# Attention and experts on one core: the experts' operations in an order read from a table, and the cast of the slots in five parts

## The chip, the cores and the metric

The program runs on one core of a Trainium2 chip. The metric is the device time of one execution in microseconds (us); lower is better. The unchanged kernel was timed three times: 1247.51, 1247.69 and 1257.23 us, median 1247.69 us.

## The reference

The program computes an attention and then a mixture of experts on its output. Queries are averaged in pairs, so 576 pooled queries meet 1152 keys, for 8 batches of 8 heads of width 64. The output, seen as 4608 tokens of width 512, goes to 8 experts. Every expert takes exactly 4608 / 8 = 576 tokens, handed out greedily from the highest gate logit down.

```python
q_pool = q.reshape(B, H, S // 2, 2, D).mean(axis=3)
attn = softmax(scale * q_pool @ k.T) @ v
x = attn.transpose(0, 2, 1, 3).reshape(4608, 512)
logits = x @ w_gate                     # 4608 x 8
for idx in argsort(-logits.flatten()):  # token idx // 8, expert idx % 8
    if token not assigned and counts[expert] < 576: assign it
for e in range(8):
    out[mask_e] = relu(x[mask_e] @ w1[e]) @ w2[e]   # 512 -> 1024 -> 512
```

## The kernel before

The program has two parts, one after the other. The attention works on 32 pairs of heads; its instructions are put in order by the class Timed, which reads a place for every operation from a table TIME. At its end VectorE (DVE) also builds the constants that the experts need. They are made by routing_tables, and one of them is slots, the numbers 0 to 639 in every row, cast from whole numbers to 16-bit floats in one instruction (L493, recorded by the helper at L475). Each of these constant operations has the tag tb and a place of its own in TIME, one every 12.98 us of the table's time.

The experts follow one another, k = 0 to 7. For each of them the kernel does three things.

**Routing** (route, L1249 to L1482). The next expert to be filled and its 576 tokens are found by a search over sorted keys in eight rounds. A round goes to and fro between DVE and TensorE (PE): DVE compares (GE, L1276), PE counts (rt<-W,GE, L1282), DVE picks its own counts (dg, red, L1285, L1287), PE adds them up (L1291), DVE compares with the room left and narrows the search (L1295 to L1301). After the rounds PE adds up once more (L1327), DVE closes the expert (L1333 to L1344) and sums (PS, tot, L1360, L1363), PE makes offsets (L1368 to L1371), DVE writes four step tables (ST, L1411), PE looks the tokens up (L1416), DVE turns that into indices (hit, idx, L1423, L1427). What the next expert's search needs is brought up to date by a count of the tokens taken (WG, ng on DVE, L1464, L1466; then PE, L1468), by U (L1476 to L1480) and by W (L1268, L1269). The routing of an expert needs the one before to be finished, so the eight of them form one chain. While expert k multiplies, the routing of expert k + 2 runs beside it.

**Fetching** (fetch). GpSimd (POOL) issues the transfers that gather by index: W1 (2 MB, L1557), five blocks of tokens (XG, L1562) and W2 (2 MB, L1557). For experts 2 to 7 DVE transposes the token blocks (XB, L1522), SyncE (SP) issues 16 small transfers that put them in place (L1529), ScalarE (ACT) and POOL split them into a high and a low 16-bit half (Xh L1541 and L1543, Xl L1547). The weights are split in the same way: ACT scales them by a power of two and casts (L1622, L1626), POOL subtracts (L1632).

**Multiplying** (ffn). PE makes 16 groups of 12 matmuls (ph, L1648), two column ranges for each of eight blocks of the hidden layer, in four banks of PSUM that are used in turn. Each group is read by ACT (relu, HX, L1653) and by DVE (the rest of it, HX, L1657, L1660). Then PE makes the output in five row blocks of 16 or 24 matmuls (po, L1675, L1678); ACT and for the last block DVE move it to SBUF (L1683 to L1689), and POOL scatters it to memory (L1695).

Every engine executes its instructions strictly in the order in which the program lists them. In the experts this order is made by the class Order. Its emit is a list scheduler: it keeps a clock for each engine, takes durations from the od.add calls, waiting times from EOWN and EWAIT, and wherever several operations could start it takes the one with the smaller priority. The priority is the operation's nominal place plus a number for its tag from ELEAD; ELATE makes a tag's result late. Matmuls of ph and po are separate operations here, so a routing instruction may stand in the middle of a group.

Tags that the change and the rows speak of: cmp (compare), pc (PE's count), own, pt (PE's sum), fa and fl (narrow), p8 (PE's last sum), cl, me, px (closing), pf (offsets), st (step tables), pl (look up), ix (indices), tk, p9 (tokens taken, and PE's count of them, L1468), lf, se, ar (CAPS, U, W), mm (ph), re (relu), rs (rest of it), m2 (po), ot, pu (output and scatter), dw, dx, dv (fetch W1, tokens, W2), xb (transpose tokens). A number ahead is the expert, a number behind counts: 3pc4 is the fifth count of expert 3.

The step that the change replaces, and the scheduler's last lines:

```python
    od = Order(ELEAD, ELATE)
    od.OWN, od.WAIT, od.switch = EOWN, EWAIT, 95
```

Of the kernel before, what the change touches and what calls it, by code (L numbers as in the profile page):

```python
# [42 lines left out]
EOWN = {"PE": 0, "ACT": 140, "DVE": 120, "POOL": 130, "SP": 60}  # L43
# [7 lines left out]
class Order:  # L51
# [10 lines left out]
    def __init__(self, lead={}, late={}):  # L62
        self.items, self.lead, self.late = [], lead, late
        self.of, self.cur, self.kind, self.stick, self.early, self.lock = [], None, [], 0, (), []
        self.switch = 83
# [97 lines left out]
class Timed(Order):  # L163
# [21 lines left out]
    def emit(self):  # L185
# [31 lines left out]
        assert done == n  # L217


AT = {"load": -15.5, "vload": -0.5, "split": -13.0, "spread": 0.5, "val": 4.0, "vs": 3.5, "vh": 5.0, "vd": 3.0, "mm":  # L220
      -3.5, "cw": 0.5093, "fold0": 3.5, "fold1": 13.1, "aug": 13.9, "lag": 3, "np": 10, "nm": 9, "stick": 0.5, "nx":
      3, "wu": 50, "pd": [11], "wv": 65, "pd0": [3, 4, 8, 9, 10, 17], "sp": 0, "d1": 2.5, "cw1":
# [217 lines left out]
def routing_tables(nc, pool, ident, jp, scratch, do):  # L440

    J = NBLK
    V = nc.vector

    def one(shape, dt, name):
        return pool.tile(shape, dt, name=name)

    C = dict(ident=ident, before=one([128, 128], BF, "before"), upto=one([128, 128], BF, "upto"),
             ones=one([128, 128], BF, "mones"), e8=one([128, J, E], BF, "e8"), pcol=one([128, 1], F32, "pcol"), pcole=one([128, 1], F32, "pcole"),
             nib=one([128, 5, 16], F32, "nib"), diag=one([128, 64], F16, "diag"), same16=one([128, 128], F16, "same16"),  # L450
             slots=one([128, 640], F16, "slots"), slot1=one([128, 5], F32, "slot1"), jval=one([128, J], F32, "jval"),
             zero=one([128, J], F32, "zero"), TAB=one([128, 2, J + 2], F16, "TAB"), pcol2=one([128, 2], F32, "pcol2"))
    it = {}
    at = 0
    for name, n in (("e8", J * E), ("p", 1), ("pe", 1), ("16", 16), ("d", 64), ("m", 128), ("s", 640), ("s1", 5), ("p2", 2)):
        it[name] = scratch[:, at:at + n]
        at += n
    it8 = it["e8"].rearrange("p (j e) -> p j e", e=E)

    def count(dur, ap, pattern, base, step):  # L460
        do("POOL", dur, lambda: nc.gpsimd.iota(ap, pattern=pattern, base=base, channel_multiplier=step))

    count(480, it8, [[0, J], [-1, E]], E, 0)
    count(80, it["p"], [[0, 1]], 0, 1)
    count(80, it["pe"], [[0, 1]], 128 * E, 1)
    count(80, it["p2"], [[1, 2]], 256 * E, 2)
    count(100, it["16"], [[1, 16]], 1, 0)
    count(210, it["d"], [[-16, 8], [0, 8]], 0, 1)
    count(240, it["m"], [[-1, 128]], 128, 1)
    count(660, it["s"], [[1, 640]], 0, 0)  # L470
    count(90, it["s1"], [[128, 5]], 1, 1)
    do("POOL", 210, lambda: (nc.gpsimd.memset(C["ones"], 1.0), nc.gpsimd.memset(C["zero"], 0.0)))

    def by(dur, f, *a, **k):
        do("DVE", dur, lambda: f(*a, **k))  # L475

    by(130, V.tensor_scalar, C["before"], jp, 0.0, None, op0=OP.is_gt)
    by(130, V.tensor_scalar, C["upto"], jp, 0.0, None, op0=OP.is_ge)
    by(220, V.tensor_copy, C["e8"], it8)
    by(62, V.tensor_copy, C["pcol"], it["p"])  # L480
    by(62, V.tensor_copy, C["pcole"], it["pe"])
    by(62, V.tensor_copy, C["pcol2"], it["p2"])
    by(62, V.memset, C["nib"], 3e9)
    for t in range(4):
        by(70, V.tensor_scalar, C["nib"][:, t, :15], it["16"][:, :15], float(16 ** t), None, op0=OP.mult)
    by(70, V.tensor_scalar, C["nib"][:, 4], it["16"], -1.0, None, op0=OP.add)
    k1 = scratch.bitcast(F32)[:, at:at + 64]
    by(90, V.tensor_scalar, k1, it["d"], 0.0, None, op0=OP.is_ge)
    by(90, V.tensor_scalar, C["diag"], it["d"], 16.0, None, op0=OP.is_lt)
    by(130, V.tensor_tensor, C["diag"], C["diag"], k1, op=OP.mult)  # L490
    by(130, V.tensor_scalar, it["m"], it["m"], 15, None, op0=OP.bitwise_and)
    by(130, V.tensor_scalar, C["same16"], it["m"], 0.0, None, op0=OP.is_equal)
    by(400, V.tensor_copy, C["slots"], it["s"])  # L493
    by(62, V.tensor_copy, C["slot1"], it["s1"])
    by(90, V.tensor_scalar, C["jval"], it["s"][:, :J], 128.0, None, op0=OP.mult)
    for z in range(2):
        by(62, V.tensor_copy, C["TAB"][:, z, J + 1:J + 2], it["p"])
    return C


def attention(ctx, tc, top, kb, sx, kt, qt, v, wg, x_dram, L, npair=NPAIR):
# [549 lines left out]
    for n in range(1, npair, 2):  # L1051
# [8 lines left out]
        else:  # L1060
# [13 lines left out]

LT = {"dve": 0, "pe": 0, "x": 8000, "w": 9900, "w0": 3700, "w1": 8000, "x0": 3000, "zd": 0, "kd": 2, "cs": 4, "wn": 4,
      "xm": 7500, "xp": 4}
ELEAD = {"ar": 4.9, "be": 51.6, "bo": 2.8, "cl": 28.5, "cmp": 29.1, "dv": 1.5, "dw": -46.1, "dx": -41.8,
# [5 lines left out]
ELATE = {"ar": -300, "bo": -300, "cl": -300, "cmp": 150, "dv": 1900, "dw": 750, "dx": 1500, "fa": -150, "fl": -300,  # L1083
# [4 lines left out]


def experts(ctx, tc, top, kb, sx, x_dram, L, w1, w2, out, C):  # L1090
    nc = tc.nc
    const = ctx.enter_context(tc.tile_pool(name="moe_const", bufs=1))
    psum = ctx.enter_context(tc.tile_pool(name="moe_psum", bufs=1, space=PSUM))
    od = Order(ELEAD, ELATE)
    od.OWN, od.WAIT, od.switch = EOWN, EWAIT, 95
    J = NBLK

    def one(shape, dt, name):
# [65 lines left out]
    re = early([128, 1], F32, "re")  # L1164
# [22 lines left out]
    ws = [x.bitcast(F32)[:, 1:2] for x in we]  # L1187
# [12 lines left out]
    rb, tb = rt[:, :128], rt[:, 128:]  # L1200
    ph = [[psum.tile([128, 512], F32, name=f"ph{i}{h}") for h in range(2)] for i in range(2)]
    po = [psum.tile([128, 512], F32, name=f"po{i}") for i in range(2)]
    V = nc.vector
# [433 lines left out]
    def ffn(k, t):  # L1637
        i = k
        for f in range(8):
            fs = slice(128 * f, 128 * f + 128)  # L1640
            for hf in range(2):
                qn = 320 if hf else 256
                qs = slice(256 * hf, 256 * hf + qn)
                p = ph[f % 2][hf][:, :qn]
                xk = [y for x in ("XH", "XL") for y in xkeys(x, 256 * hf, 256 * hf + qn)]
                for z, (d, a, b) in enumerate((d, a, b) for d in range(4) for a, b in ((W1h, Xh), (W1h, Xl), (W1l, Xh))):
                    def mm(fs=fs, qs=qs, p=p, z=z, d=d, a=a, b=b):
                        nc.tensor.matmul(p, a[:, d, fs], b[:, d, qs], start=z == 0, stop=z == 11)  # L1648
                    od.add(t + 0.5, "PE", 138 if hf else 111, mm, r=xk + [(x, f // 2, y) for x in ("W1H", "W1L") for y in range(2)],
                           w=[("ph", f % 2, hf)], tag="mm")  # L1650

                def relu(qs=qs, f=f, p=p):
                    nc.scalar.activation(HH[:, f, qs], p, AF.Relu)  # L1653

                def rest(hf=hf, qs=qs, f=f, p=p):
                    h = HH.bitcast(F32)[:, f, qs]
                    V.scalar_tensor_tensor(HL[:, f, 64 + 256 * hf:320 + 256 * hf], p[:, :256], 0.0, h[:, :256],  # L1657
                                           op0=OP.max, op1=OP.subtract)
                    if hf:
                        V.scalar_tensor_tensor(HL[:, f, :64], p[:, 256:], 0.0, h[:, 256:], op0=OP.max, op1=OP.subtract)  # L1660
                pk, hk = [("ph", f % 2, hf)], [("HH", f, hf)]
                od.add(t + 0.5, "ACT", 334 if hf else 282, relu, r=pk, w=hk, tag="re")
                od.add(t + 0.5, "DVE", 470 if hf else 335, rest, r=pk + hk, w=[("HL", f, hf)], tag="rs")
# [97 lines left out]
```

## Time and profile before

| | us |
|---|---|
| median of three runs | 1247.69 |
| the profiled execution | 1246.02 |
| its span, first to last instruction | 1243.9 |
| PE busy | 1178.5 |
| DVE busy | 986.0 |
| POOL busy | 897.3 |
| ACT busy | 867.1 |

The profiled execution took 1246.02 us, and its span on the core is 1243.9 us. Times below count from the first instruction of that span. The attention runs to 750 us, the experts from there on. PE is the busiest engine; an engine that waits while PE is fed costs nothing. [...]

### The profile page before, as it was taken

The page shows a single profiled execution, that of the slowest core. Times are in us where ns is not written, and L with a number is a line of the kernel's source. Part 1 is how long each engine was busy: PE and PEld are TensorE (multiplying, and loading weights), DVE is VectorE, ACT ScalarE, POOL GpSimd, SP SyncE. Part 2 cuts the span into 40 slices and gives each one's busy share as a digit, 9 for nine tenths or more (in the row PEclk, how much of TensorE's full clock was granted, in tenths as well). Part 3 has the DMA queues.
Part 4 walks back from the last instruction along what each step waited for, and adds up shares of the span by engine and source line. Part 5 has one row for each costly group of instructions (what it writes and reads, how often), then busy time and mean ns, then how long its engine had stood idle before and what let it go on. Part 6 is the DMA issues. An engine that isn't in the chain of part 4 may idle for free.

```text
span 1243.9 us, 37266 instructions
## 1 busy us (share of the span) xinstructions
PE 1178.5 (95%) x14875; PEld 808.1 (65%) x14875; DVE 986.0 (79%) x2323; ACT 867.1 (70%) x1603; POOL 897.3 (72%) x913
## 2 busy tenths in 40 slices
PE   8899999999999999999999996899889999999998
PEld 5566666665666666666666674676667677787776
DVE  8999999999999999999999837888776767761320
ACT  6787887886887878788788660647556464667631
POOL 4688888888788888888887980456475756668641
PEclk8899999999999999999999998999899999999999
DMA  7564675666465576567565300542443436253411
GB/s 224 146 180 122 159 180 138 168 162 146 126 168 140 153 179 159 124 163 181 136 171 128 94 2 20 174 184 83 133 157 120 152 108 215 86 183 118 141 39 38
DMA packets 95692, 171.07 MB, mean 138 GB/s; under 512 B 17694, under 2 KB 54558, under 8 KB 93342
## 3 DMA queue, kind: packets, MB, share of 16 engines
q1 hardware_dynamic: 82574, 107.09, 32.0%
q0 software_dynamic: 12800, 61.58, 16.5%
q8 instruction: 117, 1.92, 0.6%
q14 instruction: 57, 0.47, 0.1%
q10 hardware_dynamic: 144, 0.02, 0.0%
HBM read 99.63 MB, written 18.87 MB: 95 GB/s over the span
## 4 chain that ended last, share of the span: by engine, by line
PE 67%; DVE 19%; issue 5%; ACT 3%; DMA 2%; POOL 2%; another core or an unknown queue 0%; SPq 0%; POOLq 0%; DVEq 0%; ACTq 0%
PE av L872 13%; PE po L1678 12%; PE ph L1648 9%; DVE MX L739 6%; PE sc L838 6%; PE sc L839 6%; PE mt L746 5%; PE kb L838 3%; PE kb L839 3%; PE av L908 3%; DVE PM L860 1%; PE mt L935 1%; POOL W2L L1632 1%; DVE V L689 1%; DMA out_dram<-OT,idx 1%
## 5 line engine op out<-in xcount | busy, mean ns | idle before, releaser
L860 POOL TENSOR_TENSOR PM<-P 128x512 f16<-128x512 f32 x537 | 586.1, 1159 | 114.8 <-ACT P L855 105.2
L739 DVE TENSOR_REDUCE MX<-mt 128x2 f32<-128x1024 f32 (+2 forms) x341 | 374.2, 1131 | 17.9 <-PE mt L746 12.3
L872 PEld LDWEIGHTS <-P 128*128 128x128 bf16 x4608 | 230.1, 98 | 61.0 <-issue 27.2
L855 ACT ACTIVATE P<-sc 128x512 f32<-128x512 f32 x384 | 224.4, 604 | 44.8 <-PE sc L839 40.5
L872 PE MATMUL av<-V,P 128*128 128x65 f16 (+1 forms) x4608 | 243.6, 193 | 1.1 <-DVE X L922 0.6
L872 PE MATMUL av<-V,PM 128*128 128x65 f16 x2304 | 235.5, 195 | 0.7 <-DVE KS L625 0.5
L872 PEld LDWEIGHTS <-PM 128*128 128x128 f16 x2304 | 212.2, 97 | 1.4 <-DVE PM L860 0.6
L839 PE MATMUL sc<-QB,KB 66*128 66x64 f16 (+2 forms) x768 | 178.5, 287 | 0.0
L838 PE MATMUL sc<-QA,KA 128*128 128x512 f16 (+1 forms) x768 | 177.1, 287 | 0.6 <-ACT P L855 0.3
L1678 PE MATMUL po<-W2H,HX 128*128 128x512 f32 x512 | 168.9, 405 | 0.7 <-DVE OT L1688 0.7
L855 ACT ACTIVATE P<-kb 128x512 f32<-128x512 f32 x192 | 115.1, 600 | 62.9 <-PE kb L839 61.4
L1648 PE MATMUL ph<-Xh,W1h 128*128 128x320 f16 (+1 forms) x512 | 147.4, 288 | 2.1 <-DVE HX L1657 1.0
L838 PEld LDWEIGHTS <-KA 128*128 128x128 f16 x1152 | 96.5, 98 | 79.2 <-issue 40.9
L1648 PE MATMUL ph<-Xl,W1h 128*128 128x320 f16 (+1 forms) x512 | 147.5, 288 | 0.5 <-DVE Xl L1512 0.5
L1648 PE MATMUL ph<-Xh,W1l 128*128 128x320 f16 (+1 forms) x512 | 147.4, 288 | 0.0
L1657 DVE SCALAR_TENSOR_TENSOR HX<-ph,HX 128x256 fp32r<-128x256 f32 x128 | 53.2, 419 | 102.4 <-ACT HX L1653 98.9
L1678 PE MATMUL po<-W2L,HX 128*128 128x512 f32 (+1 forms) x320 | 127.9, 400 | 0.0
L1632 POOL TENSOR_TENSOR W1l<-W,W1h 128x512 f16<-128x512 f32 x62 | 72.1, 1165 | 77.2 <-ACT W1h L1626 74.0
L1653 ACT ACTIVATE HX<-ph 128x256 fp32r<-128x256 f32 (+1 forms) x128 | 51.5, 409 | 103.6 <-PE ph L1648 96.0
L1648 PEld LDWEIGHTS <-W1h 128*128 128x128 f16 x1024 | 99.1, 98 | 35.3 <-issue 9.8
L839 PEld LDWEIGHTS <-KB 66*128 66x128 f16 (+1 forms) x1152 | 94.9, 98 | 37.3 <-issue 2.4
L1678 PEld LDWEIGHTS po<-W2H,HX 128*128 128x128 f32 x512 | 94.4, 190 | 17.6 <-DVE OT L1688 1.1
(270 smaller groups left out, 2279.2 us busy)
## 6 DMA issues: line engine op xcount, KB each, us to landing
KD<-in_kt_dram SPq DMA_DIRECT2D x64, 288.0 KB
VD<-in_v_dram SPq DMA_DIRECT2D x32, 576.0 KB
QA<-QH SPq DMA_DIRECT2D x128, 72.0 KB
KA<-KH SPq DMA_DIRECT2D x64, 144.0 KB
KB<-KH SPq DMA_DIRECT2D x64, 144.0 KB
KA<-KL SPq DMA_DIRECT2D x64, 144.0 KB
x_dram<-X SPq DMA_DIRECT2D x16, 576.0 KB
QS<-in_qt_dram SPq DMA_DIRECT2D x31, 288.0 KB
```

The lines of the kernel that those rows point to most:

```text
L739: od.add(t, "DVE", d, lambda: nc.vector.tensor_reduce(dst, src, axis=AX.X, op=OP.max), r=[f"m{m}"], w=w, tag="mr", k=z)
L746: nc.tensor.matmul(mt[s][:, y], pairs[b][s], KH[i][h, ks], start=True, stop=True)
L838: nc.tensor.matmul(c, KA[i][:, s, ks], QA[i][:, s, qs], start=first, stop=False, skip_group_check=True)
L839: nc.tensor.matmul(c, KB[i][:kr, s, ks], QB[i][:kr, s, qs], start=False, stop=last, skip_group_check=True)
L855: od.add(g + 0.1, "ACT", 480, lambda: nc.scalar.activation(p, c, AF.Exp, scale=1.0 / UNIT), r=[ck], w=[("P32", g % NP)], tag="exp", k=g % ...
L860: od.add(g + 0.2, en, dur, lock=1, fn=lambda: eng.tensor_tensor(pm, p, hi, op=OP.subtract), r=[("P32", g % NP)], w=[("PM", g % NM)], tag=" ...
L872: nc.tensor.matmul(out, w[:, qs], v, start=kb == 0 and j == 0 and y == 0, stop=kb == NKB - 1 and y == 2, skip_group_check=True)
L1632: eng.tensor_tensor(o, a, b, op=OP.subtract), r=[key] + sr + [(nm + "H", z, y)], w=[(nm + "L", z, y)], first=first, lock=1, tag="wl" if nm ...
L1648: nc.tensor.matmul(p, a[:, d, fs], b[:, d, qs], start=z == 0, stop=z == 11)
L1653: nc.scalar.activation(HH[:, f, qs], p, AF.Relu)
L1657: V.scalar_tensor_tensor(HL[:, f, 64 + 256 * hf:320 + 256 * hf], p[:, :256], 0.0, h[:, :256], op0=OP.max, op1=OP.subtract)
L1678: nc.tensor.matmul(o[:n], a[:, z, q0:q0 + n], b[:, z], start=z == 0 and y == 0, stop=z == 7, skip_group_check=True)
```

## The change

The class Order is replaced, for the experts, by a class Listed. It collects the operations by name. A name is the expert, the tag and a running number; the 12 matmuls of a ph group have one name, and 6 matmuls of po have one name, so these now stay together. The operations are then emitted in the order of their numbers in the table ETIME, except that none is emitted before the operations it depends on. ELEAD and ELATE go. One line of the table stands in the diff as an example (the place of 5mm15 is on its next line):

```diff
+class Listed(Order):
+    def add(self, t, eng, dur, fn, r=(), w=(), late=0, first=0, tag=None, kind=0, lock=None, k=None):
+        Order.add(self, t, eng, dur, fn, r, w, late, first, tag, kind, lock, k)
+        self.names.append((int(t // 10), tag or {"PE": "pe", "DVE": "dv", "POOL": "po", "ACT": "ac", "SP": "sp"}[eng] + "_"))
+
+    def emit(self):
...
+            name = f"{k}{tag}{z // {'mm': 12, 'm2': 6}.get(tag, 1)}"
...
+        heap = [(self.table[made[i][0]], i) for i in range(n) if not left[i]]
+        heapq.heapify(heap)
...
+            _, i = heapq.heappop(heap)
+            for fn in made[i][1]:
+                fn()
...
-    by(400, V.tensor_copy, C["slots"], it["s"])
+    for c in range(5):
+        by(100, V.tensor_copy, C["slots"][:, 128 * c:128 * c + 128], it["s"][:, 128 * c:128 * c + 128])
...
+         346253, "5re13": 354527, "5rs13": 355006, "5mm14": 347909, "5re14": 354861, "5rs14": 355476, "5mm15":
...
-    od = Order(ELEAD, ELATE)
-    od.OWN, od.WAIT, od.switch = EOWN, EWAIT, 95
+    od = Listed(ETIME)
```

In the attention, the cast of slots is now five instructions of 128 columns. TIME gets four more places (2tbw to 2tbz), so the five casts stand one every 12.98 us of the table's time, and the four small constants behind them move back by four places. The rest of the attention keeps its order.

In the experts all engines are reordered. Three places follow, each before and after. A name in capitals is a tile; the number after an underscore tells apart tiles of one kind; numbers behind a name are its shape.

First DVE, where it gets the routing of expert 3 ready while expert 1 multiplies. HX with 128x256 or 128x64 is the rest of a ph group of expert 1, W is what PE's first count of expert 3 needs beside GE, GE is the compare. Before:

```order
L1660 SCALAR_TENSOR_TENSOR HX<-ph_14630,HX 128x64
L1230 TENSOR_REDUCE kb<-T_14555 128x36
L1471 TENSOR_TENSOR CAPS<-CAPS,rt 128x8
L1472 SCALAR_TENSOR_TENSOR CAPS<-kb,CAPS 128x8
L1657 SCALAR_TENSOR_TENSOR HX<-ph_14627,HX 128x256
L1305 TENSOR_SCALAR kb<-kb,base 128x36
L1476 SCALAR_TENSOR_TENSOR U<-kb,U 128x36
L1478 SCALAR_TENSOR_TENSOR room<-PS,of,kb 128x36
L1479 TENSOR_TENSOR kb<-room,kb 128x36
L1480 TENSOR_TENSOR U<-U,kb 128x36
L1268 TENSOR_TENSOR ru<-kb,U 128x36
L1269 TENSOR_TENSOR W<-kb,ru 128x288
```

After:

```order
L1572 TENSOR_REDUCE kb<-LM 128x36
L1581 TENSOR_SCALAR ki<-kb 128x36
L1573 TENSOR_TENSOR T_14559<-LM,kb 128x288
L1583 TENSOR_TENSOR kb<-ki,kb 128x36
L1574 TENSOR_TENSOR T_14559<-T_14559,kb 128x288
L1575 TENSOR_REDUCE kb<-T_14559 128x36
L1613 TENSOR_TENSOR ru<-kb,U 128x36
L1614 TENSOR_TENSOR W<-kb,ru 128x288
L1584 TENSOR_SCALAR ki<-kb 128x36
L1585 MEMSET base 128x1
L1585 CAST kb<-ki 128x36
L1621 SCALAR_TENSOR_TENSOR GE<-kb,base,nib 128x576
```

Before, the rest of group 12 of expert 1 (HX from ph_14627) stands between GE (above these rows) and W. After, all sixteen of expert 1 stand ahead of W, and GE comes behind W.

Then PE at the end of the routing of expert 3: the look-up of the tokens (rt<-TAN,ST), the count of the tokens taken (rt<-ng) and the ph groups of expert 2. Before:

```order
L1416 LDWEIGHTS ST
L1416 MATMUL rt<-TAN,ST 128x38
L1416 LDWEIGHTS ST
L1416 MATMUL rt<-TAN,ST 128x38
L1468 LDWEIGHTS mones
L1468 MATMUL rt<-ng,mones 128x8
L1648 LDWEIGHTS W1h
L1648 MATMUL ph_14627<-Xh,W1h 128x256
```

After:

```order
L1993 LDWEIGHTS W1h
L1993 MATMUL ph_14631<-Xl,W1h 128x256
L1993 LDWEIGHTS W1l
L1993 MATMUL ph_14631<-Xh,W1l 128x256
L1813 LDWEIGHTS mones
L1813 MATMUL rt<-ng,mones 128x8
L1993 LDWEIGHTS W1h
L1993 MATMUL ph_14632<-Xh,W1h 128x320
```

Before, the count stands right behind the look-up and ahead of the first ph matmul of expert 2. After, five ph groups of expert 2 stand ahead of it (four before the look-up and one between). The same engine's last eight rounds of expert 3 also lie elsewhere: before, its first count stands in the last ph group of expert 1; after, it stands behind that group and five groups of 6 po matmuls, and of the rest of expert 1's po matmuls 10 stand between the fifth and the sixth count, 6 between the sixth and the seventh, none between the seventh and the eighth, and 6 behind the eighth; the ph groups of expert 2 come only after the offsets (pf) of expert 3.

Last POOL, where it fetches for expert 3. Before:

```order
L1557 DMA W1_14598<-in_w1_dram,widx3_14593 128x4096
L1547 TENSOR_TENSOR Xl_14620<-XG_14617,Xh_14619 128x4x4x32
L1632 TENSOR_TENSOR W2L_14616<-W2_14599,W2H_14615 128x512
L1547 TENSOR_TENSOR Xl_14620<-XG_14617,Xh_14619 128x4x4x32
L1632 TENSOR_TENSOR W2L_14616<-W2_14599,W2H_14615 128x512
L1562 DMA XG_14617<-x_dram_67,idx3_14584 128x512 x4
L1562 DMA XG_14617<-x_dram_67,idx3_14584 64x512
L1632 TENSOR_TENSOR W2L_14616<-W2_14599,W2H_14615 128x512 x6
L1694 MEMSET spacer_14635 1x1
L1695 DMA out_0_dram<-OT2_14625,idx1_14582 4608x512
L1557 DMA W2_14599<-in_w2_dram,widx3_14593 128x4096
```

After:

```order
L1902 DMA W1_14602<-in_w1_dram,widx3_14597 128x4096
L2039 MEMSET spacer_14639 1x1
L2040 DMA out_0_dram<-OT2_14629,idx1_14586 4608x512
L1977 TENSOR_TENSOR W2L_14620<-W2_14603,W2H_14619 128x512 x3
L1902 DMA W2_14603<-in_w2_dram,widx3_14597 128x4096
L1907 DMA XG_14621<-x_dram_67,idx3_14588 128x512 x2
L1907 DMA XG_14621<-x_dram_67,idx3_14588 64x512
L1907 DMA XG_14621<-x_dram_67,idx3_14588 128x512 x2
```

Before, the five blocks of tokens are issued ahead of W2; after, behind it. For expert 2 the same holds; for experts 4 to 7 the tokens stay ahead of W2. At the program's end, the last output block is the fourth (which ACT alone moves to SBUF) in place of the fifth (which ACT and then DVE move).

## Rows read from the trace of the kernel before

**Rows 1.** The page: the span, and the engines' busy time.
```profile
span 1243.9 us, 37266 instructions
PE 1178.5 (95%) x14875; PEld 808.1 (65%) x14875; DVE 986.0 (79%) x2323; ACT 867.1 (70%) x1603; POOL 897.3 (72%) x913
```

**Rows 2.** Windows: us, busy PE, PEld, DVE, ACT, POOL (x), clock, DMA, GB/s.
```profile
856.00:921.00 65.00, 56.74 (x404) 41.10 (x402) 51.80 (x221) 38.56 (x73) 42.24 (x44) 0.94 0.45 152
975.00:1031.00 56.00, 53.69 (x384) 40.08 (x383) 40.88 (x164) 33.50 (x64) 36.40 (x40) 1.00 0.40 133
1088.00:1139.00 51.00, 51.00 (x357) 40.73 (x357) 19.96 (x85) 33.77 (x65) 34.98 (x36) 1.00 0.45 145
```

**Rows 3.** Waits of PE, 786 to 1244 us: us in total, times, longest.
```profile
PE rt L1282 <- DVE W L1269: 6.4, 3, 3.1
PE rt L1468 <- DVE idx L1427: 3.9, 3, 2.6
PE rt L1282 <- DVE GE L1276: 1.8, 4, 0.6
PE rt L1291 <- DVE red L1287: 1.8, 3, 0.9
PE ph L1648 <- DVE HX L1657: 1.0, 1, 1.0
...
PE rt L1327 <- DVE full L1295: 0.8, 1, 0.8
PE rt L1368 <- DVE tot L1363: 0.7, 1, 0.7
```

**Rows 4.** By tile: the cast of slots, and a constant of 128x128: ns, start.
```profile
L475 DVE CAST slots<-scratch x1: 4001/4001/4001, 306.8 to 306.8; 128x640 f16<-128x640 int32 x1
L475 DVE TENSOR_SCALAR same<-scratch x1: 600/600/600, 292.4 to 292.4; 128x128 f16<-128x128 int32 x1
```

**Rows 5.** Timeline of PE behind that cast: start, us, line, [idle before <-releaser].
```profile
312.70 1.54 PE L935 MATMUL mt<-ident,X 128*128 128x128 f32 x6 [3.34 <-DVE MX L739]
```

**Rows 6.** Windows at half clock, columns as in rows 2.
```profile
312.60:316.00 3.40, 3.30 (x42) 3.24 (x43) 3.40 (x4) 2.52 (x5) 1.38 (x1) 0.50 0.10 15
...
882.70:889.50 6.80, 5.31 (x25) 3.45 (x24) 4.70 (x20) 4.49 (x11) 0.00 (x0) 0.50 0.54 229
...
920.50:923.50 3.00, 2.98 (x15) 2.09 (x15) 2.86 (x14) 1.33 (x4) 2.07 (x3) 0.50 0.39 120
```

**Rows 7.** Timeline of PE: the first and the last step of expert 3's routing.
```profile
884.19 0.42 PE L1282 MATMUL rt<-W,GE 128*128 128x64 bf16 x5 [3.08 <-DVE W L1269]
...
920.51 0.17 PE L1468 MATMUL rt<-ng,mones 128*128 128x8 bf16 x1 [2.62 <-DVE idx L1427]
```

**Rows 8.** Timelines at 876 us: last matmul of group 12, its relu, W.
```profile
876.07 0.27 PE L1648 MATMUL ph<-Xh,W1l 128*128 128x256 f16 x1
...
881.55 0.38 ACT L1653 ACTIVATE HX<-ph 128x256 fp32r<-128x256 f32 x1 [5.30 <-remote]
...
883.67 0.46 DVE L1269 TENSOR_TENSOR W<-kb,ru 128x288 bf16<-128x288 f32 x1
```

**Rows 9.** Timeline of PE: one round of a routing with nothing else beside it.
```profile
761.89 0.32 PE L1282 MATMUL rt<-W,GE 128*128 128x64 bf16 x5 [0.48 <-DVE GE L1276]
...
762.82 0.17 PE L1291 MATMUL rt<-red,same 128*128 128x8 f16 x1 [0.24 <-DVE red L1287]
...
764.58 0.32 PE L1282 MATMUL rt<-W,GE 128*128 128x64 bf16 x5 [0.48 <-DVE GE L1276]
```

**Rows 10.** The chain that ended last: 76 po matmuls with nothing between.
```profile
1117.92 17.37 PE po L1678 x76
```

**Rows 11.** Windows, columns as in rows 2: a load of W2.
```profile
1052.00:1060.00 8.00, 8.00 (x68) 6.34 (x66) 3.64 (x15) 2.32 (x7) 0.00 (x0) 1.00 0.77 279
```

**Rows 12.** Timeline at the end: the last output block, on ACT, then DVE.
```profile
1238.20 0.68 ACT L1686 ACTIVATE O<-po,wf 64x512 f32<-64x512 f32 x1 [2.97 <-PE po L1678]
1238.91 0.74 DVE L1688 SCALAR_TENSOR_TENSOR OT<-po,wf,O 64x512 f32<-64x512 f32 x1 [25.17 <-ACT O L1686]
```

More of the change, by code (lines that the diff above doesn't have):

```diff
@@ L217, in emit, with __init__ @@
         assert done == n
+class Listed(Order):
+    def __init__(self, table):
+        Order.__init__(self)
+        self.table, self.names = table, []
+    def add(self, t, eng, dur, fn, r=(), w=(), late=0, first=0, tag=None, kind=0, lock=None, k=None):
+        Order.add(self, t, eng, dur, fn, r, w, late, first, tag, kind, lock, k)
+        self.names.append((int(t // 10), tag or {"PE": "pe", "DVE": "dv", "POOL": "po", "ACT": "ac", "SP": "sp"}[eng] + "_"))
+    def emit(self):
+        group, made, seen = {}, [], {}
+        for i in sorted(range(len(self.items)), key=lambda i: (self.items[i][0], i)):
+            k, tag = self.names[i]
+            z = seen[k, tag] = seen.get((k, tag), -1) + 1
+            name = f"{k}{tag}{z // {'mm': 12, 'm2': 6}.get(tag, 1)}"
+            if name not in group:
+                group[name] = len(made)
+                made.append((name, [], [], []))
+            _, fns, r, w = made[group[name]]
+            fns.append(self.items[i][4])
+            r.extend(x for x in self.items[i][5] if x not in r)
+            w.extend(x for x in self.items[i][6] if x not in w)
+        n, writer, readers = len(made), {}, {}
+        need = [set() for _ in range(n)]
+        for i, (_, _, r, w) in enumerate(made):
+            for k in r:
+                if k in writer:
+                    need[i].add(writer[k])
+                readers.setdefault(k, []).append(i)
+            for k in w:
+                if k in writer:
+                    need[i].add(writer[k])
+                need[i].update(readers.get(k, ()))
+                readers[k] = []
+                writer[k] = i
+            need[i].discard(i)
+        users, left = [[] for _ in range(n)], [len(x) for x in need]
+        for i, x in enumerate(need):
+            for j in x:
+                users[j].append(i)
+        heap = [(self.table[made[i][0]], i) for i in range(n) if not left[i]]
+        heapq.heapify(heap)
+        done = 0
+        while heap:
+            _, i = heapq.heappop(heap)
+            for fn in made[i][1]:
+                fn()
+            done += 1
+            for j in users[i]:
+                left[j] -= 1
+                if not left[j]:
+                    heapq.heappush(heap, (self.table[made[j][0]], j))
+        assert done == n
@@ L1076 @@
       "xm": 7500, "xp": 4}
-ELEAD = {"ar": 4.9, "be": 51.6, "bo": 2.8, "cl": 28.5, "cmp": 29.1, "dv": 1.5, "dw": -46.1, "dx": -41.8,
[5 rows of a table removed]
-ELATE = {"ar": -300, "bo": -300, "cl": -300, "cmp": 150, "dv": 1900, "dw": 750, "dx": 1500, "fa": -150, "fl": -300,
[4 rows of a table removed]
+ETIME = {"0be0": 0, "0be1": 580, "0be2": 1100, "0be3": 1620, "0ke0": 490, "0ke1": 950, "0ke2": 1470, "0ke3": 1990,
[298 rows of a table added]
 def experts(ctx, tc, top, kb, sx, x_dram, L, w1, w2, out, C):
@@ L1649, in ffn @@
                     od.add(t + 0.5, "PE", 138 if hf else 111, mm, r=xk + [(x, f // 2, y) for x in ("W1H", "W1L") for y in range(2)],
-                           w=[("ph", f % 2, hf)], tag="mm")
+                           w=[("ph", f % 2, hf)], tag="mm", kind=1)
                 def relu(qs=qs, f=f, p=p):
```

309 rows, old and new, of tables (ELATE, ELEAD, ETIME, TIME) are left out of this document.

## The prediction

> **What bounds the kernel now.** I read the page's engine table first. TensorE is busy for 1178.5 of 1243.9 us [rows 1], so everything any order can win lies in the 65 us in which it is not busy, and in the matmuls that run at half clock. Then I read the windows, one per expert. The stretch from 1088 to 1139 has PE busy for all of its 51.00 us at clock 1.00, and there is nothing to gain there; the stretch from 856 to 921 takes 65.00 us for the same kind of work, 8.3 us of them without PE, at a mean clock of 0.94 [rows 2]. So the early experts are where an order matters, and the later ones are already bound by PE.
>
> Third, PE's waits from the experts' first ph matmul on [rows 3]. By rows: W 6.4 us in three waits, idx (which holds up the count of tokens taken) 3.9 in three, GE 1.8, red 1.8, HX 1.0, full 0.8, tot 0.7. Together 16.4 us. All but HX are links of the routing chain, which goes to and fro between DVE and PE: PE executes in order, so a routing matmul that comes too early in its queue stops the big matmuls behind it.
>
> Fourth, the timeline at the longest of these. PE stands 3.08 us at the first count of expert 3, for W, and 2.62 us at its last count, for idx [rows 7]. Why W is late stands at 876 us [rows 8]: the last matmul of ph group 12 ends at 876.07 + 0.27 = 876.34, but ACT's relu of that group starts at 881.55, 5.21 us later, after an idle time of 5.30. Its releaser is shown as remote, which names no engine, and I cannot say what held ACT. On DVE the rest of that group stands ahead of W in the queue, so W is made at 883.67 and PE's count at 884.19. The routing did not need the group; it was only queued behind it. [...]
>
> In the attention the cast of slots holds DVE for 4.00 us [rows 4], and PE then waits 3.34 us for MX, DVE's next product [rows 5]. The 3.30 us of work behind that run at 0.50 too [rows 6]: 1.65 us lost.
>
> **The change, part by part.** The sums are made against the profiled execution, 1246.02 us; the median of the runs is 1247.69, so 1.67 is added at the end.
>
> *The cast.* Removed: 3.34 + 1.65 = 4.99. Added: five casts of 128 columns. A fifth of 4.00 is 0.80; the operation of 128x128 in rows 4 took 0.60. Of the 4.00 us, 4.00 − 3.34 = 0.66 did not reach PE, so a piece of 0.60 would be hidden and one of 0.80 would show 0.14. Bounds: nothing, and five times 0.60 = 3.0 if no slack is there. I take 0.2 each, 1.0 in all. Net −3.99. The four constants behind it move back, but are needed only when routing begins at 750 us.
>
> *W of expert 3.* In the new DVE order all sixteen rests of expert 1 stand ahead of W, and PE has five groups of 6 po matmuls ahead of the first count. 76 of these took 17.37 us, 0.2286 each [rows 10], so the thirty are 6.9 us of work that stands in front of the count and covers even a relu that is 5.21 late. The 3.08 go, and with them the 2.65 of the clock. The other W waits (6.4 − 3.08 = 3.32) and HX's 1.0 come, I suppose, from late relus too; nothing in the order makes a relu punctual, so I let them stay.
>
> *The count of tokens taken.* In three experts PE waits for idx, 3.9 in all. Now one more ph group stands between look-up and count in expert 3. Sixteen groups, the routing between them and 112 po matmuls (25.6 us) fill the 51.00 us of a full expert, so a group is about (51.00 − 25.6) / 16 = 1.59 us. That covers only part of 2.62, but the four groups ahead of the look-up also give DVE work time, as the step tables are then long ready. I take all 3.9 off, and 1.49 of clock.
>
> *The rounds.* GE, red, full and tot make 5.1 us. A group of 12 or 6 kept whole between two steps gives a constant cover, and I take off half: 2.55. *The end.* The last block now leaves by ACT alone; DVE's 0.74 behind ACT's 0.68 [rows 12] goes. Sum of what goes in the experts: 3.08 + 2.65 + 3.9 + 1.49 + 2.55 + 0.74 = 14.41.
>
> *What comes.* Between the last rounds of expert 3 PE now has little. In a bare round [rows 9] PE counts at 761.89 for 0.32, sums at 762.82 for 0.17 and counts again at 764.58: it waits 0.61 and then 1.59. Fifth round: 0.61, and ten po matmuls (2.29) cover the rest. Sixth: 0.61, and six (1.37) leave 0.22. Seventh, with nothing: 0.61 + 1.59. Eighth: 0.61, then the last sum and the offsets, for which I take the full 0.8 and tot 0.7 of rows 3. Together 0.61 + 0.83 + 2.20 + 0.61 + 1.5 = 5.75. With gaps this close a fall of the clock is likely; the nearest row is the 2.98 us window, 1.49. And in several places a bank of PSUM is used again with one other ph group between instead of three. If relu and rest are prompt this costs nothing; one relu as late as rows 8 would cost 5.21 − 1.59 = 3.62. I take 1.0, between nothing and 3.62. Added: 5.75 + 1.49 + 1.0 = 8.24.
>
> Experts: −14.41 + 8.24 = −6.17. All: −3.99 − 6.17 = −10.16, so 1235.9 on the profiled basis and **1237.5 us** on that of the median, 0.8% less. A difference of about 1% is what a measurement of this kernel can tell from none, so this is just inside "within 1%".
>
> *POOL's order* I cost at nothing, but it is the most doubtful place. For experts 2 and 3 the tokens are now issued behind W2 (2 MB). Such a load moved at 279 GB/s [rows 11], 7.5 us, so the tokens may land that much later. What hides it: the tokens of expert 3 are multiplied only when expert 2's 51 us of work are over. What is queued behind: on DVE the transposes of the token blocks wait for the landing, and behind them stand compares and rests; on POOL the Xl of the same tokens. No row of before shows tokens behind a W2.
>
> [...]
>
> **The rivals.**
>
> A: the new order works wherever the old one waited. Then all of rows 3 (16.4) goes, the clock's 2.65 + 1.49, the 0.74 and the whole 4.99 of the cast: 26.27. If half of the bare rounds' 5.75 stays, it is 1246.02 − 26.27 + 2.88 = 1222.6, and 1224.3 on the median's basis. For it: experts at 51.00 us with PE never idle exist in this trace [rows 2], so they are possible. Against it: the late relus, whose cause is not in the order of any queue that I can read.
>
> B, the slower side: tokens of experts 2 and 3 come too late behind W2. DVE stops at their transposes, the rests behind them wait, PE stops for want of a bank. Price: 7.5 us each, and each stop brings a clock fall like that of the first window, 2.65: 20.3 us. With the rest of the forecast 1235.9 + 20.3 = 1256.2, or 1257.8, slower by 0.8%. It decides from the point at which the tokens land after DVE has reached the first transpose of that expert. For: tokens demonstrably later in the queue. Against: POOL issues ahead of use by a large part of an expert.
>
> C: the experts gain nothing. One relu as late as that of rows 8 in a place where its bank is soon used again costs 3.62 and a clock fall of 2.65, 6.27 us, as much as the 6.17 forecast. Then only the cast's 3.99 is left: 1242.0, or 1243.7. For: such relus exist in before. Against: only one of them is known to be that late.
>
> **How the numbers follow.** Forecast 0.43, with its own range from 1231 (the cast's casts hidden, no clock fall, no loss at the banks: 1.0 + 1.49 + 1.0, and the other half of the rounds' 5.1) to 1245 (the cast at 3.0, the banks at 3.62, the idx waits only by half: 2.0 + 2.6 + 2.7 with its clock). A 0.27, C 0.20, B 0.10. Faster by over 1% means below 1235.2: all of A but a little, 0.25, and two fifths of the forecast's own range, 0.17, so 0.42. Slower by over 1% means above 1260.2: B with somewhat more than its price, 0.08. The rest, 0.50, is within. The range leaves out the better part of A below 1226 and most of B above 1253.
>
> **What would show it.** In the changed kernel's timeline, near the casts of slots, no PE wait over 0.5 us and clock 1.00. No wait for W at expert 3's first count, and none over 1 us at its last. PE waits of 0.6 to 1.6 us for GE, red, full and tot between expert 1's last po matmuls and expert 2's first ph matmul, perhaps with the clock at 0.50. The window of 65.00 us down to about 58. At the end no DVE operation behind ACT's. The prediction is wrong if DVE's transposes in experts 2 and 3 are released by a transfer while PE stands (B), if waits for HX appear in ph (C), or if PE's waits from 786 us on sum to under 4 us (A).

## The result and the profile after

The change makes the kernel slower. Over 22 runs each, the median goes from 1249.79 to 1260.51 us; the ratio is 1.0069, with a 95% interval from 1.005 to 1.0087 (the medians alone give 1.0086). The forecast was 1237.5 us and faster. The profiled execution of the changed kernel took 1255.26 us, span 1253.4, so it lies below that median; it is 9.2 us above the profiled execution of before.

The attention ends at nearly the same time in both (last av matmul at 745.6 us before, 746.1 after). So 8.7 of the 9.2 us lie in the experts, and the gain that the cast should have brought is not there.

PE's waits in the experts, as [rows 3] (us in total, times, longest):

```profile
PE rt L1636 <- DVE red L1632: 7.9, 9, 2.4
PE po L2020 <- ACT OT L2028: 7.3, 3, 4.8
PE rt L1627 <- DVE GE L1621: 3.4, 3, 1.6
PE po L2023 <- ACT OT L2028: 2.9, 3, 1.2
PE rt L1713 <- DVE tot L1708: 1.7, 1, 1.7
PE rt L1813 <- issue: 1.2, 2, 0.6
PE rt L1813 <- DVE idx L1772: 0.9, 1, 0.9
PE po L2023 <- ACT OT L2029: 0.8, 1, 0.8
PE ph L1993 <- DVE HX L2002: 0.7, 2, 0.4
```

W, the largest row of before with 6.4 us, is gone. The count of tokens taken (L1813) is down from 3.9 to 2.1. The rows of the rounds (red, GE, tot) have grown. And there is a new thing, OT: PE's output groups wait 7.3 + 2.9 + 0.8 = 11.0 us for ACT to move an earlier output block out of the bank that they need.

The windows, as [rows 2], taken where the same experts lie now (us, busy PE, PEld, DVE, ACT, POOL, the granted clock of PE as a share of full speed, DMA, GB/s):

```profile
854.00:921.00 67.00, 56.41 (x407) 41.96 (x405) 52.36 (x218) 42.23 (x79) 49.35 (x52) 0.97 0.35 124
979.00:1036.00 57.00, 53.35 (x391) 40.86 (x390) 41.97 (x165) 32.61 (x61) 37.57 (x42) 1.00 0.46 151
1098.00:1149.00 51.00, 45.82 (x286) 36.26 (x284) 14.91 (x55) 33.30 (x62) 34.12 (x40) 0.97 0.52 164
```

The first window is no better than before. The third is the surprise: before, PE was busy for all 51.00 us there; now it is idle for 5.2. The timelines of PE and ACT show what happened (start, us, engine and line, [idle before <-releaser]). PE:

```profile
1139.56 0.79 PE L2020 MATMUL po<-W2H,HX 128*128 128x512 f32 x1 [4.78 <-ACT OT L2028]
```

ACT, around the same time:

```profile
1128.02 0.69 ACT L2028 ACTIVATE OT<-po,wf 128x512 f32<-128x512 f32 x1 [0.67 <-issue]
...
1131.04 0.82 ACT L1888 CAST Xh<-XG 128x512 f16<-128x512 f32 x2
1137.55 0.72 ACT L1886 ACTIVATE XG<-XG,sx 128x512 f32<-128x512 f32 x1 [5.69 <-DMA XG<-XB]
1138.30 0.62 ACT L1888 CAST Xh<-XG 128x512 f16<-128x512 f32 x1
1138.83 0.68 ACT L2028 ACTIVATE OT<-po,wf 128x512 f32<-128x512 f32 x1
```

PE waits for the OT at 1138.83. ACT is not busy: it stands 5.69 us for the small transfers that put the tokens of expert 6 in place (XG<-XB), and the OT, which needs nothing of those tokens, is the next in its queue. In the packets of the trace those transfers run from 1113.8 to 1136.7 us, 22.9 us; in before the same 16 ran from 1112.7 to 1122.2, 9.5 us. Beside them now run W2 of expert 6, issued at 1113.4, and W1 of expert 7, issued at 1126.9. Before issued the first at 1104.7, ahead of the transfers, and the second at 1134.2, behind them. Of the 1280 data packets of the transfers 1024 had gone by 1128.7; the last 256 ran from 1132.2 to 1136.7, beside those of W1 (1128.6 to 1135.8). PE's clock is then at 0.50 from 1139.1 for 3.4 us.

The rounds of expert 3 do stand bare, as forecast. Timeline of PE:

```profile
907.47 0.17 PE L1636 MATMUL rt<-red,same 128*128 128x8 f16 x1 [0.61 <-issue]
...
910.82 0.17 PE L1636 MATMUL rt<-red,same 128*128 128x8 f16 x1 [0.61 <-DVE red L1632]
...
913.53 0.17 PE L1636 MATMUL rt<-red,same 128*128 128x8 f16 x1 [0.62 <-DVE red L1632]
915.29 0.32 PE L1627 MATMUL rt<-W,GE 128*128 128x64 bf16 x5 [1.60 <-DVE GE L1621]
916.23 0.17 PE L1636 MATMUL rt<-red,same 128*128 128x8 f16 x1 [0.61 <-DVE red L1632]
916.66 0.17 PE L1672 MATMUL rt<-full,mones 128*128 128x8 bf16 x1 [0.27 <-DVE full L1640]
...
920.83 0.16 PE L1713 MATMUL rt<-tot,before 128*128 128x2 bf16 x1 [1.71 <-DVE tot L1708]
```

0.61 + 0.61 + 0.62 + 1.60 + 0.61 + 0.27 + 1.71 = 6.03 us; the prediction had 5.75 for these. Behind the sixth of these, from 917.2 us, the clock is at 0.50 for 6.8 us.

The cast of slots, as [rows 4] and [rows 5]: the tile's row, then PE's wait:

```profile
L532 DVE CAST slots<-scratch x5: 211/647/3744, 309.2 to 362.1; 128x128 f16<-128x128 int32 x5
```

```profile
314.93 0.88 PE L993 MATMUL mt<-ident,X 128*128 128x128 f32 x6 [3.08 <-DVE MX L797]
```

The first of the five, a fifth of the work, took 3.74 us where the whole took 4.00, and PE waited 3.08 where it had waited 3.34.

### The profile page after: what moved, and what is told of

It is laid out like the page before. It is cut to its first block, busy times and chain, and to the rows that moved or that the text cites. A ratio compares the mean times of both kernels' runs of the same rounds, so it can differ in the third digit from the quotient of the medians.

```text
span 1253.4 us, 37175 instructions
## 1 busy us (share of the span) xinstructions
PE 1178.0 (94%) x14875; PEld 811.6 (65%) x14875; DVE 988.5 (79%) x2327; ACT 869.2 (69%) x1603; POOL 898.6 (72%) x913
## 5 line engine op out<-in xcount | busy, mean ns | idle before, releaser
L2023 PE MATMUL po<-W2H,HX 128*128 128x512 f32 x512 | 172.2, 402 | 3.7 <-ACT OT L2028 2.9
L1993 PEld LDWEIGHTS <-W1h 128*128 128x128 f16 x1024 | 96.4, 98 | 32.3 <-issue 8.1
L1998 ACT ACTIVATE HX<-ph 128x320 fp32r<-128x320 f32 (+1 forms) x128 | 50.4, 409 | 89.8 <-PE ph L1993 68.7
L2002 DVE SCALAR_TENSOR_TENSOR HX<-ph,HX 128x256 fp32r<-128x256 f32 x128 | 52.0, 416 | 75.0 <-ACT HX L1998 71.7
L2040 POOL DMA_INDIRECT out_dram<-OT,idx x40 | 38.9, 973 | 91.0 <-ACT OT L2028 54.0
```

The costliest lines, as they stand in the source:

```text
L2023: nc.tensor.matmul(o[:n], a[:, z, q0:q0 + n], b[:, z], start=z == 0 and y == 0, stop=z == 7, skip_group_check=True)
L2040: st = nc.gpsimd.indirect_dma_start(out=out, out_offset=bass.IndirectOffsetOnAxis(ap=idx[i][:n, c:c + 1], axis=0), in_=OT[ob][:n], in_offs ...
```

## The experiments

Two things were to be told apart: why the cast still stalls, and whether the experts lost their gain to the OT that stands behind late transfers, or to the bare rounds, or to the tokens behind W2 (rival B). The runs were taken on three other chips, each with the kernel before beside them, and the ratios are to that. On these chips the kernel before took 1235.6 to 1236.9 us; in none of the twelve traces from them does a relu wait with the releaser remote as in [rows 8], and PE's wait for W is 0.3 us in e1, where it was 6.4.

**e1: the five casts alone, in the kernel before.**

```diff
-    by(400, V.tensor_copy, C["slots"], it["s"])
+    for c in range(5):
+        by(100, V.tensor_copy, C["slots"][:, 128 * c:128 * c + 128], it["s"][:, 128 * c:128 * c + 128])
```

> The kernel before, with only the cast of slots in five parts. Theory size (the step of my prediction): the 4.00 us belong to the 640 columns; the first part takes 0.6 to 0.8 us, PE's wait of 3.34 us for MX is gone, and the time falls by about 4 us (0.3%). Theory burst: the cast waits until POOL's run of seven PM products is over, whatever its width; then the first part takes 3.5 to 4 us again, PE waits about 3 us again, and the time is the same within 1 us but for the clock.

Measured: 1235.38 us, ratio 0.9992 [0.998, 1.0004]: no change. The timelines of DVE and POOL show why:

```profile
306.16 7.23 POOL L861 TENSOR_TENSOR PM<-P 128x512 f16<-128x512 f32 x7
...
309.75 3.74 DVE L475 CAST slots<-scratch 128x128 f16<-128x128 int32 x1
```

The cast starts inside POOL's run of seven PM products and ends at 313.49; the run ends at 313.39. In the kernel after it is the same: the run ends at 312.89, the cast at 312.97.

**e2: the cast in one piece, a few places later on DVE.**

```diff
-"2tbr": 253260
+"2tbr": 258460
```

> The kernel before, with the cast of slots in one piece, only placed a few DVE instructions later, behind the two MX that PE waits for and behind POOL's run of seven PM products. Theory size: it still takes about 4 us on DVE, wherever it stands. Theory burst: it takes about 1 us (five times 0.2), PE's wait of 3.34 us is gone, and the time falls by 3 to 5 us.

Measured: 1232.69 us, ratio 0.997 [0.9957, 0.9983]. By tile:

```profile
L475 DVE CAST slots<-scratch x1: 476/476/476, 318.1 to 318.1; 128x640 f16<-128x640 int32 x1
```

All 640 columns take 0.48 us; PE's wait for MX is gone. So of the 4.00 us of [rows 4], 3.5 were a wait for POOL. Theory burst holds. In the trace of before the cast runs from 306.75 to 310.75, and POOL's run of seven products, 7.23 us, ends at 310.39. So it waited not for one product (7.23 / 7 = 1.03 us) but for the rest of the run.

**e3: in the kernel after, W1 of expert 7 is issued behind the last Xl of expert 6.**

```diff
+ETIME.update({"7dw0": 371000})
```

> The kernel after, with the load of W1 of expert 7 issued behind the last Xl of expert 6, as before has it. Theory transfers: that load and W2 hold up the 16 small transfers that put expert 6's tokens in place (22.9 us in after, 9.5 in before); ACT waits 5.7 us for them and OT, which PE needs, stands behind. Then the transfers end by about 1130, PE's wait of 4.78 us at 1139 falls below 2, the clock does not fall there, and the time is 3 to 6 us lower. Theory order of ACT: the transfers are late anyhow through W2, and the wait stays above 3 us.

Measured: 1247.22 us, ratio 1.0092 [1.0074, 1.0109]. The transfers of expert 6 take 14.4 us in place of 22.9, the long wait at the end of expert 5 is gone, and the five runs lie within 3.8 us. By itself this trace doesn't show that W1's place did it, since in e5 below the transfers are as short and the wait is gone without the move. Against the ratio that e5 below gives for after it is 0.35% less, some 4 us, though the intervals overlap and the chips differ. The other waits for OT stayed (2.9, 2.6 and 1.7 us), so after remained slower than before.

**e4: in the kernel after, OT ahead of the steps it was queued behind.**

```diff
+ETIME.update({"1ot2": 145104, "3ot0": 250520, "4ot0": 304559, "5ot2": 365272, "6ot0": 408196, "0pu0": 116961})
```

> The kernel after, with six numbers of the table changed, so that ACT moves an output block to SBUF ahead of the two weight steps or the token step behind which it was queued (experts 1, 3, 4, 5, 6), and POOL scatters the first block of expert 0 ahead of the load of W1 of expert 2. Theory order of ACT: PE's waits for OT, 11.0 us in all, fall below 3, with the clock fall behind the longest 8 to 12 us of the time. Theory transfers alone: only the longest falls, some 5 us, as the others are hidden or come back as waits for Xh. If neither is the cause, the time stays at that of after.

Measured: 1243.02 us, ratio 1.0046 [1.0024, 1.0067]; the runs fall into two groups, 1235 to 1238 and 1241 to 1246. The numbers for 5ot2 and 6ot0 moved nothing, since their own matmuls stand later in the table. So the waits for OT in experts 0, 1 and 3 and the larger one in expert 4 went; that of expert 5 stayed (4.5 us; transfers 22.6 us), and that of expert 6 (0.8).

**e5: the kernel after once more.**

> The kernel after, unchanged, timed beside the others of this call, as the chips differ. If the waits for OT and the bare rounds are set by the order, they are in this trace at the same places and sizes (PE's waits for OT near 11 us with the longest at the end of expert 5, six waits of 0.6 to 2.7 us in the last rounds of expert 3); if they were an accident of one execution, they are elsewhere or gone. Ratio to before 1.005 to 1.009.

Measured: 1250.76 us, from 1243.28 to 1256.99, ratio 1.0127 [1.0098, 1.0156]. The profiled execution was the shortest, and in it the transfers of expert 6 took 14.5 us and the end of expert 5 has no wait, at the same issue times as in the first trace (W2 0.4 us ahead of the first transfer, W1 13.1 behind it). All packets of the transfers had gone by 1123.1, and the first of W1 came at 1123.4; in the first trace a fifth of them were still to go when W1's began. So the long wait is a race that goes one way or the other with the same order. It is one reason why after spreads over 14 us: the two groups of e4, in which of the larger waits only this one was left, lie some 8 us apart. The rest of the spread isn't explained. The bare rounds and the other waits for OT were where they had been:

```profile
PE po L2023 <- ACT OT L2028: 2.9, 3, 1.2
PE po L2020 <- ACT OT L2028: 2.6, 2, 2.0
...
PE po L2023 <- ACT OT L2029: 2.0, 1, 2.0
```

**e6: e3 and e4 together, and the token steps of experts 6 and 7 behind the OT.**

```diff
+ETIME.update({"1ot2": 145104, "3ot0": 250520, "4ot0": 304559, "0pu0": 116961, "7dw0": 371000, "6xh2": 367551, "7xh3": 410314, "7xh2": 410324})
```

> The kernel after with e3 and e4 together; and as OT of expert 5's third block can't go ahead of its own matmuls, the token step of expert 6 that it stood behind now stands behind it (for expert 6 and 7 the same). Theory that the waits for OT and the transfers behind W1 are what the experts lost: PE's waits for OT fall below 2 us in all, no clock fall near the end of expert 5, and the time is 8 to 12 us below after, so at that of before or 2 us under it. Theory that the bare rounds of expert 3 are the larger part: 3 to 6 us below after, and still above before.

Measured: 1237.39 us, ratio 1.0009 [0.9992, 1.0026], within 6.5 us. One wait for OT is left, 0.5 us. Against e5 on the same chip it is 13.4 us less: changing the places of a few OT, one scatter, one load and three token steps gives the whole loss of the change back. Of these 13.4 the two profiled executions show 6.7 (1243.28 to 1236.61), with PE's waits for OT down by 7.0 (7.5 to 0.5). The rest fits the long wait, which e5's profiled execution didn't have and its longer runs may have had; no trace of these shows it. The bare rounds are all still there:

```profile
PE rt L1636 <- DVE red L1632: 4.8, 8, 0.9
PE rt L1627 <- DVE GE L1621: 2.2, 2, 1.6
...
PE po L2020 <- ACT OT L2028: 0.5, 1, 0.5
```

**e7: as e6, with po groups between the bare rounds of expert 3.** On DVE, W and GE of expert 3 go ahead of 1rs14, 1rs15 and 1rs12; on PE the order becomes:

```
1m24 1m25 1m20 1m21 3pc0 1m22 3pt0 1m23 3pc1 1m26 1m27 3pt1 1m28 3pc2 1m29 3pt2 1m210 3pc3 1m212 3pt3
1m211 3pc4 1m213 3pt4 3pc5 1m216 3pt5 1m217 3pc6 3pt6 3pc7 1m218 3pt7 1m214 3p80 1m215 3pf0
```

> As e6, and the routing of expert 3 begins about 2 us sooner (on DVE W and GE stand ahead of the last three rests of expert 1) and gets its po matmuls where the rounds were bare: four groups of six instead of five ahead of its first count, one each between the later rounds. If the bare rounds cost what my prediction put on them (5.75 us and a clock fall of 1.5), it is 4 to 8 us faster than e6. If they are only a symptom of a chain that DVE sets, the waits move elsewhere and it is within 2 us of e6.

Measured: 1240.41 us, ratio 1.0023 [1.0008, 1.0039], 3 us above e6. The rows moved: red from 4.8 down to 3.0, GE from 2.2 up to 4.6, tot from 1.2 up to 2.6, and a wait of 1.08 for WQ (at 892.68 us) has come, so 3.5 for WQ in all. From the first count to the offsets the chain took 33.9 us, where e6 took 30.6. So in this order the po matmuls between the rounds moved the waits and lengthened the chain. It was slower than either theory had it; that DVE's steps set the length of the chain is argued, not shown.

**e8: the kernel before, with the cast as in e2 and the count of tokens taken of experts 3 to 5 14 ph matmuls later.**

```diff
-        for i in order:
+        [(order.remove(i), order.insert(min(order.index(j) for j in users[i]), i)) for i in order[:] if getattr(items[i][4], "behind", 0)]
+        for i in order:
...
+            count.behind = 3 <= k <= 5
```

> The kernel before with the cast of slots moved as in e2, and the count of tokens taken of experts 3, 4 and 5 put 14 ph matmuls later. If that count's waits (2.8, 0.9 and 0.9 us) are worth their size, it is 3 to 5 us below e2, so 6 to 9 us below before (0.5% to 0.7%). If the next routing is late by as much in their place, it is at the time of e2 (0.3% below before).

Measured: 1231.29 us, ratio 0.9955 [0.9939, 0.997], the fastest of all. PE's waits:

```profile
PE rt L1282 <- DVE W L1269: 3.5, 4, 2.2
PE rt L1282 <- DVE GE L1276: 1.8, 4, 0.6
```

The 3.9 us for idx are gone, and 3.5 us for W, the first count of the next search, have come (0.3 in e2). The clock fall at that place (914.5 us in e2) is gone as well. The ratio lies between the two theories: 0.45% below before, where e2 alone was 0.3%.

**e9: as e6, but W1 of expert 7 issued early, as in after.**

```diff
-"0pu0": 116961, "7dw0": 371000,
+"0pu0": 116961,
```

> As e6, but W1 of expert 7 is issued where after has it, ahead of the Xl of expert 6. Theory that it takes both, the late transfers and an OT queued behind the step that waits for them: the late transfers then hold nothing that PE needs at once, and the time is that of e6 within 2 us, with a narrow spread of the runs. Theory that the collision costs by itself: some of the runs are 4 to 8 us longer, as in after and e4, and the median is 3 us or more above e6.

Measured: 1235.44 us, ratio 0.9991 [0.9976, 1.0006], within 7.2 us. With the OT in front, the early load costs nothing that can be seen. In the one profiled execution the transfers took 14.7 us, so it doesn't show a long one being hidden; that is argued from the narrow spread of the runs.

**e10: as e6, with the tokens of experts 2 and 3 ahead of W2.**

```diff
+ETIME.update({..., "2dv0": 130300, "3dv0": 177950})
```

> As e6, but the tokens of experts 2 and 3 are issued ahead of W2, as in before. The rival B of my prediction (tokens late behind W2 stop DVE) gives a gain of several us over e6. By the trace of after, in which DVE has no wait ahead of the transposes of experts 2 and 3, the time is that of e6 within 2 us.

Measured: 1243.13 us, ratio 1.0057 [1.0038, 1.0076]: 0.5% slower than e6, the opposite of rival B. The timelines of POOL, ACT and PE:

```profile
883.36 0.96 POOL L1902 DMA_INDIRECT W<-in_w_dram,widx  x1 [0.30 <-issue]
884.32 0.09 POOL L2039 MEMSET spacer<- 1x1 f32 x1
884.62 0.99 POOL L2040 DMA_INDIRECT out_dram<-OT,idx  x1 [0.22 <-issue]
```

```profile
893.66 0.69 ACT L2028 ACTIVATE OT<-po,wf 128x512 f32<-128x512 f32 x1 [3.70 <-DMA out_dram<-OT,idx]
...
901.90 0.68 ACT L2028 ACTIVATE OT<-po,wf 128x512 f32<-128x512 f32 x1
```

```profile
902.63 0.49 PE L2020 MATMUL po<-W2H,HX 128*128 128x512 f32 x1 [2.80 <-ACT OT L2028]
```

W2, issued later, now has a scatter right behind it. The scatter's 9 us to landing (884.62 to 893.66) keep an OT buffer, of which there are three; ACT waits 3.70, the next OT starts at 901.90, where e6 has 898.75, and PE waits 2.80. In e6, with W2 issued ahead of the tokens and the scatter, the OT that waits here starts at 890.11 with no wait. In e10 the packets of W2 run from 885.0 to 892.6, and the scatter's first packet moves at 890.96, 6.3 us after its issue. The tokens in after started late as well: those of expert 2, issued from 879.38 on behind W2, have their first packet at 884.30, 4.9 us later; in e10, with W2 behind them, it comes 1.7 us after their issue. What holds the packets behind a W2 back is not shown. But in after the tokens had landed by 890.2, and DVE came to their transposes at 891.99.

**e11: e6 with the cast as in e2.**

```diff
-    for c in range(5):
-        by(100, V.tensor_copy, C["slots"][:, 128 * c:128 * c + 128], it["s"][:, 128 * c:128 * c + 128])
+    by(400, V.tensor_copy, C["slots"], it["s"])
...
-"2tbr": 253260
+"2tbr": 258460
```

> As e6, with the cast of slots in one piece and behind POOL's run of PM products, as in e2. If the two gains add, it is 3 to 4 us below e6, so about 0.3% below before.

Measured: 1233.68 us, ratio 0.9976 [0.9958, 0.9995]. The two add up.

**e12: e8 without the cast.**

```diff
-"2tbr": 258460
+"2tbr": 253260
```

> The kernel before with only the count of tokens taken of experts 3 to 5 put 14 ph matmuls later (e8 without the cast). If these waits are worth their size and the clock fall behind the longest, 3 to 5 us below before (ratio 0.996 to 0.9975). If the next search only waits in their place, ratio 0.999 to 1.001.

Measured: 1234.28 us, ratio 0.9987 [0.9969, 1.0005]. The interval holds both theories; what the count's place is worth by itself, at most some 4 us, stays open. PE's waits for idx are gone and for W are 3.5, as in e8.

## Why the prediction was wrong

- **The step that failed is one that was not in the sum: ACT's order.** The prediction went through DVE, PE and POOL, and put 1.0 us (up to 3.62) on PSUM banks that are used again soon, all of it in ph. The waits for HX in ph came to 0.7 us by L2002 and 0.4 by L2005, so that term was not the miss. The two banks of po were not looked at: who frees them is OT on ACT, and what stands ahead of OT in ACT's new queue was never read. There were 11.0 us of waits, and a clock fall of 3.4 us at 0.50 behind the longest. e6 takes all but 0.5 us of them away, and the time is that of before again.
- **The cast (−3.99): wrong.** The duration was read as work, divided by five, and the slack of 0.66 was compared with the parts. It was a wait for POOL of 3.5 us that the cast met at that place whole or in parts, and not a few places later (e1, e2). The small operation of 0.600 us in [rows 4], which the estimate leaned on, stood at another place. The clock did stay at 1.00 behind the cast in after, so the 1.65 us (an estimate, half of the 3.30 in [rows 6]) went there; but a fall of 3.4 us stands at 29.8 us that before doesn't have, in e1 the clock falls behind the cast again (316.7), and the attention ended no sooner.
- **W of expert 3 (−3.08): right here, and more.** All three W waits went, 6.4 us in all, where 3.32 had been left in. On the other chips there was nothing to win: 0.3 us in e1.
- **The count of tokens taken (−3.9): half.** 2.1 us are left, and e8 and e12 show that putting it off mostly moves the wait to the next search.
- **The rounds (−2.55, +5.75).** The bare rounds of expert 3 were nearly right in sum, 6.03 us against 5.75, in part by luck: full took 0.27 where 0.8 had been put, tot 1.71 where 0.7 had. The half of 5.1 that was to go from the others did not: red, GE and tot together are 13.0 us in after, 5.15 of them in the bare rounds (the sixth 0.61 is listed as issue), so 7.85 elsewhere; 2.44 of these are one wait at 994 us, where ACT and DVE both stand with the releaser remote. In e5, whose trace has no such waits, red, GE, tot and full come to 9.2 us, not far from the 8.3 that the sum left for them (2.55 + 5.75); in after they come to 13.5. "A group kept whole gives a constant cover" was argued, and is not what the trace shows.
- **The clock (−2.65 −1.49 +1.49): it came out even,** where 2.65 us had been forecast as gain. No run shows these terms: they are the author's estimate, half of the 5.31 and 2.98 us that PE is busy in the windows of [rows 6]. What the trace of after shows in their place is that po matmuls follow one another every 0.43 us at 0.50 (1140.15 to 1142.29) and every 0.23 at 1.00 (1142.63 to 1144.95). Before had 6.8 and 3.4 us at 0.50 in the experts behind the first, after has the same, at other places. One fall stands behind the longest wait (4.78 us), the other behind the bare rounds, where no single wait is over 1.71; the single wait of 2.44 us at 994 us has none.
- **The end (−0.74): right**, with 0.6: from the last po matmul to the end 6.1 us before and 5.5 after.

Rival B named nearly the size that came, 0.8% slower, but its mechanism is refuted: DVE has no idle time (the last column) ahead of the ten transposes of experts 2 and 3 in after, by lines from 880 to 1000 us, and undoing it costs time (e10).

```profile
L1867 DVE STREAM_TRANSPOSE XB<-XG 128x512 f32<-128x512 f32 (+1 forms) x10 | 6.8, 692 | 0.0
```

Rival C is too small and names another mechanism: it put the experts at no gain, 1243.7 us with the cast's gain, and they lost 8.7 us. No late relu is needed for the loss, since it is larger (1.27%) in e5, whose trace has none. Rival A is refuted by the result.

## What to carry to other kernels

When an order is replaced, read for each engine what now stands ahead of the operations that free a buffer for the busiest engine; in after ACT, busy for 869.2 of 1253.4 us, still delayed them, as it waited 5.69 us for a transfer in between, and PE then 4.78. A long duration of a small operation on DVE may be a wait, as 3.5 of the cast's 4.00 us were: look at what POOL does from its start to its end, and compare with the same operation elsewhere, before its size is divided. A large transfer put ahead of small ones, or of a scatter whose buffer is soon needed, is priced by who stands behind these, not by its own lateness: with W2 ahead of the scatter in e10, ACT waited 3.70 us and PE 2.80.

## What the runs showed of the hardware that was not expected

- A cast from 32-bit whole numbers to 16-bit floats waited on DVE until POOL's whole run of products was over (3.74 us for 128 columns, 0.21 to 0.79 for the next four, 0.48 for 640 columns behind the run).
- Sixteen small transfers took 9.5 us with a 2 MB load issued 8 us ahead of them, and 14.5 or 22.9 us with one issued at their start and a second 13 us later; which of the two differed between executions of the same program with the same issue times to 0.1 us. While the first load moved, from 1115 to 1121 us in the first trace, 88 of their 1280 packets went.
- Relus that wait with the releaser remote, up to 5.21 us late, occur in the traces of both kernels on the first chip, and in none of the twelve from the three others. What holds ACT there stays open; it wasn't tried.
